# First block's second layer in seven block products, with weight sums prepared in four tiles and a newly computed order list

## The chip, the cores and the metric

The kernel runs on one core of one Trainium2 chip. The metric is the device time of that core in microseconds (us), a median over runs. TensorE (PE) multiplies, VectorE (DVE) and ScalarE (ACT) work on vectors, GpSimd (POOL) reduces over partitions and issues the large weight loads, SyncE (SP) issues smaller transfers.

## What is computed

Attention with a window of 64 positions, then two layers of a feed-forward network with a leaky rectifier between them, all in 32-bit floats:

```
scores = scale * q @ k.T            # 8 batches, 8 heads, 576 positions, head size 64
mask   = (rel >= 0) & (rel < 64)    # rel = query position - key position
attn   = softmax(where(mask, scores, -1e9));  x = (attn @ v) as 4608 tokens x 512
h = x @ w_in                        # 512 x 2048
g = maximum(0.01 * h, h)
out = g @ w_out                     # 2048 x 512
```

## The kernel before, in words

Every 32-bit number is held as a high and a low part, and a product is three matmuls of 128x128 weights on 128x512 columns (high by high, high by low, low by high). The attention works in 36 **units** of 128 queries, numbered m. The 4608 tokens are 9 chunks of 512: chunks 0 to 2 go through both layers plainly, and the other six are three **blocks** s = 0, 1, 2 of two chunks each.

The first layer of a block (lines 1318 to 1355, names `m0` to `m2`) is computed in seven products of half-size blocks in place of eight, which takes sums of weight blocks and of x blocks made beforehand. The second layer of blocks 1 and 2 (`second_in_seven`, line 1229, names `z1`, `z2`, line 1186) does the same with sums of the intermediate g and of `w_out`. The second layer of block 0 (lines 1361 to 1382, function `second`, line 1132, name `y0`) is computed plainly: 2 chunks by 16 slices of g by 4 output tiles by 3 matmuls.

In a second layer, ACT copies a wide piece of g (128x1024) into the high part of a *pair* tile (`wide_high`, line 1163), DVE writes the low part (`wide_low`, line 1167), and PE multiplies by it. In `y0` a pair serves 24 matmuls and there are two pair tiles (`gs` and `pxa`); in `z1` and `z2` a pair serves 12 matmuls and there are three (`third` besides). DVE also adds pieces of g there (`combine`, line 1170).

The sums of weights are made in `prepare` (line 1013): a fetch of the parts, on DVE one wide addition of high and low (line 1033, for `w_out` alone), four narrow additions (line 1036), a copy on ACT (line 1039), a subtraction on DVE (line 1042), a store. For `w_in` the fetch is of the whole numbers (`w_single`, stored by `split`, line 247, as the weights are converted at the start), for `w_out` of high and low parts (`w_second`).

A unit of the attention goes: scores on PE (line 278); mask on DVE (line 666, `shield_of`); for units from 20 on the result stays in the accumulator bank and ACT copies it (line 672, `held_back`); maximum over partitions on POOL (line 681); subtraction on DVE (line 688); exponential on ACT (line 692); sum on POOL (line 684); and the values on PE (line 740). Then come three transfers in a row on SP: the sums are compacted (`late_c<-late_o`, line 695), written as rows after a reciprocal (`rows<-late_c`, line 716) and spread again (`late_r<-rows`, line 728). The **normalisation** `product_of` (line 752, DVE) waits for the last of them, and its result is stored for the next block's x (`x_build`, line 852, loads it back and makes the sums of x).

From the start to the first layer of chunk 0 an order written out by hand is followed (`ORDER`, line 54). All later work is a list of operations, each with an engine, a duration and a rank; `arrange` (line 544) walks through it once, always taking the ready operation of lowest rank, and every engine executes its instructions in the order that comes out. Ranks of late units carry an added 0.45, and the waits of their transfers extra lags, for instance `lag=0.3 + 6 * late` before the normalisation (line 837).

Of the kernel before, what the change touches and what calls it, by code (L numbers as in the profile page):

```python
# [38 lines left out]
PACE = 2  # L39
LANES = 8  # L40
# [44 lines left out]
RING_AT = (5, 6, 7, 8)  # L85
HELD_FROM = 20
IN_PREP_AT = (0, 0, 0, 6, 7, 0, 6, 7)
OUT_PREP = 0.6
IN_SEVEN = (1, 2)
# [15 lines left out]
def band_attention_ffn(ctx: ExitStack, tc: tile.TileContext, qk, vW, vL, w_in, w_out, eye_mask, out, outT):  # L105
# [89 lines left out]
    w_single = dram.tile([FT, P, 512], F32, name="w_single")  # L195
# [336 lines left out]
    def op(engine, us, fn, *after, rank=1.0, lag=0.12, land=0.0):  # L532
        x = dict(engine=engine, us=us, fn=fn, after=[a for a in after if a], rank=rank, lag=lag, land=land, n=len(plan))
        plan.append(x)
        return x
# [8 lines left out]
    def arrange():  # L544
        free, left = dict.fromkeys(("PE", "DVE", "ACT", "POOL", "SP"), 0.0), list(plan)
        waiting = {e: [] for e in free}
        missing, users = {}, {}
        for x in plan:
            missing[x["n"]] = len(x["after"])
            for a in x["after"]:  # L550
                users.setdefault(a["n"], []).append(x)
            if not x["after"]:
                waiting[x["engine"]].append((0.0, x))
        order, landed = [], [0.0] * LANES

        def begins(ready, x):
            return max(ready, landed[0]) if x["land"] and x["engine"] != "POOL" else ready

        while any(waiting.values()):
            best = None  # L560
            for e, xs in waiting.items():
                if xs:
                    t = max(free[e], min(begins(*y) for y in xs))
                    if best is None or t < best[0]:
                        best = t, e
            t, e = best
            r, x = min((y for y in waiting[e] if begins(*y) <= t), key=lambda y: (y[1]["rank"], y[1]["n"]))
            waiting[e] = [y for y in waiting[e] if y[1] is not x]
            free[e] = t + x["us"]
            x["end"] = free[e] + x["land"]  # L570
# [4 lines left out]
            for y in users.get(x["n"], ()):  # L575
                missing[y["n"]] -= 1
                if not missing[y["n"]]:
                    at = max(a["end"] + (0.0 if a["engine"] == y["engine"] and not a["land"] else y["lag"]) for a in y["after"])
                    waiting[y["engine"]].append((at, y))
        assert len(order) == len(plan)  # L580
        return order

    MM, TWO, ONE, ACTS = 0.2267, 1.05, 0.72, 0.62
# [3 lines left out]
    XT_AT, PREP_AT = 4, 6  # L587
# [36 lines left out]
    turn_of = [15, 14, 13, 12] + list(range(12))  # L624
# [28 lines left out]
    stored = [(f, fn) for f in turn_of for fn in stores_of(f)]  # L653
# [14 lines left out]
    def held_back(m):  # L668
        return m >= HELD_FROM
# [101 lines left out]
    def attend(m, gate):  # L771

        soon = 0.35 if early(m) else 1.3
        o, late = at.setdefault(m, {}), 0.0 if early(m) else 0.45
# [23 lines left out]
        for j in range(2):  # L798
            o[f"A{j}"] = op("POOL", 3.5, partial(add_of, m, j), o[f"X{j}"], before.get(f"c{j}"), rank=0.4 + late)
# [7 lines left out]
    def normalise(m):  # L807

        late = 0.0 if early(m) else 0.45
        soon = 0.15 if early(m) and m > 13 else 0.8 + late  # L810
# [41 lines left out]
    def x_build(s, n, xt_of, xt_free, x_free):  # L852

        STEP, WIDTH = (0.42, 0.27) if s == 2 else (0.5, 0.35)
        urge, wait = ((0.2, 0.2), (1.4, 2.6), (0.6, 2.6))[s]
# [118 lines left out]
    for n, (c, f) in enumerate(walk):  # L974
        next_main(6 * MM, partial(early_first, n, 0), lows.get(n - 2), *ready[f], *(x2 if c == 2 else ()))
        first = next_main(6 * MM, partial(early_first, n, 1))
        if n == 0:
# [5 lines left out]
            gate = op("SP", 0.02, open_room, *all_in, s_free)  # L983
        if n > 1:
# [28 lines left out]
    def prepare(n, f, at, hurry, *freed):  # L1013
        def tile_of():
            return g_tile(at) if at else hold("spare", F32)
# [441 lines left out]
```

## Time and profile before

| what | value |
|---|---|
| median of 3 runs | 849.75 us (849.49 to 850.38) |
| span of the profiled execution | 849.6 us |
| PE busy | 842.2 us (99%), 6784 matmuls |
| DVE busy | 621.6 us (73%) |
| ACT busy | 375.3 us (44%) |
| POOL busy | 383.1 us (45%) |
| granted TensorE clock | full in every slice |
| moved by DMA | 226.80 MB, mean 267 GB/s |

A busy share is an average over stages with different limits. A span of a few hundred nanoseconds on PE is one matmul's time from issue to end, and neighbours overlap; the chain of waits gives the time from one to the next.

### The profile page before, as it was taken

The numbers are of one execution on the slowest core, as the hardware profiler recorded it, in microseconds if no ns is written. First come the engines' busy times: TensorE is split into PE (matmuls) and PEld (weight loads), VectorE is DVE, ScalarE is ACT, GpSimd is POOL, SyncE is SP. The second block draws the span as 40 slices with busy tenths as digits, with TensorE's granted clock in tenths as the row PEclk, the third lists the DMA queues.
The fourth block names the chain that finished last, engine by engine and source line by source line (L and its number), as shares of the span: only waits on it lengthen the run. The fifth ranks groups of instructions, "written<-read, shape, count | busy, mean of one in ns | idle before, by whom it ended". The sixth has DMA issues, their size and how long they took to land.

```text
span 849.6 us, 16804 instructions
## 1 busy us (share of the span) xinstructions
PE 842.2 (99%) x6784; PEld 686.8 (81%) x6784; DVE 621.6 (73%) x884; ACT 375.3 (44%) x605; POOL 383.1 (45%) x218
## 2 busy tenths in 40 slices
PE   9999999999999999999999999999999999999998
PEld 6887888888878888878888888888888888888887
DVE  6999885748768879857649977585679955546864
ACT  4665654333433444444444433444354533324431
POOL 5423000878888715578577857857111111111110
PEclk9999999999999999999999999999999999999999
DMA  9874756898899968999999999999997987777682
GB/s 326 271 235 146 252 165 232 264 289 269 283 318 323 306 200 286 298 309 329 320 328 364 375 355 316 361 317 304 247 270 234 248 247 199 198 197 192 192 214 96
DMA packets 127901, 226.80 MB, mean 267 GB/s; under 512 B 15568, under 2 KB 46672, under 8 KB 127824
## 3 DMA queue, kind: packets, MB, share of 16 engines
q0 software_dynamic: 51552, 90.18, 38.4%
q10 hardware_dynamic: 35664, 77.31, 27.8%
q1 hardware_dynamic: 40608, 58.24, 21.5%
q8 instruction: 53, 0.87, 0.4%
q14 instruction: 24, 0.20, 0.1%
HBM read 172.52 MB, written 53.06 MB: 266 GB/s over the span
## 4 chain that ended last, share of the span: by engine, by line
PE 91%; DVE 4%; DMA 4%; issue 0%; ACT 0%; SPq 0%; ACTq 0%; DVEq 0%
PE m L1118 25%; PE z L1186 18%; PE acc L929 11%; PE h L920 11%; PE y L1138 10%; PE h L431 4%; PE acc L467 4%; PE s L278 4%; PE o L740 3%; DMA late_r<-rows 1%; DMA raw<-w_out 1%; DMA rows<-late_c 1%; DMA raw<-w_in 1%; PE o L367 1%; DVE w L242 1%; DMA w_single<-w 0%
## 5 line engine op out<-in xcount | busy, mean ns | idle before, releaser
L1118 PE MATMUL m<-pfew,p 128*128 128x512 f32 x720 | 169.4, 391 | 0.0
L1118 PEld LDWEIGHTS m<-pfew,p 128*128 128x128 f32 x720 | 134.5, 188 | 28.3
L1102 POOL DMA_DIRECT2D p<-w_first x42 | 31.7, 755 | 114.2 <-PE m L1118 62.4
L929 PE MATMUL acc<-p,gs 128*128 128x512 f32 x324 | 80.6, 394 | 0.0
L1127 DVE TENSOR_TENSOR p<-m,pxa 128x512 f32<-128x512 f32 x60 | 41.4, 689 | 45.6 <-PE m L1118 45.2
L681 POOL PARTITION_ALL_REDUCE g<-late_f x20 | 36.8, 1874 | 79.4 <-DVE late_f L666 71.6
L1118 PE MATMUL m<-pxb,p 128*128 128x512 f32 x288 | 71.0, 392 | 0.7 <-DVE pxa L1127 0.7
L684 POOL PARTITION_ALL_REDUCE late_o<-late_f x20 | 65.3, 3290 | 11.6 <-ACT late_f L692 7.1
L929 PEld LDWEIGHTS acc<-p,gs 128*128 128x128 f32 x324 | 59.8, 188 | 12.8
L1130 ACT ACTIVATE p<-p 128x512 f32<-128x512 f32 x60 | 37.9, 631 | 72.7 <-DVE p L1127 72.5
L1127 DVE TENSOR_TENSOR pxa<-m,pxa 128x512 f32<-128x512 f32 x60 | 41.4, 689 | 37.1 <-PE m L1118 36.4
L1118 PEld LDWEIGHTS m<-pxb,p 128*128 128x128 f32 x288 | 53.6, 188 | 12.4 <-DVE pxa L1127 1.1
L684 POOL PARTITION_ALL_REDUCE late_o<-e x18 | 59.6, 3343 | 8.5 <-ACT e L692 4.1
L684 POOL PARTITION_ALL_REDUCE late_o<-late_e x18 | 59.2, 3315 | 5.8 <-ACT late_e L692 5.6
L1186 PE MATMUL z<-gs,p 128*128 128x512 f32 (+1 forms) x240 | 57.2, 386 | 0.0
L1102 POOL DMA_DIRECT2D p<-w_second x28 | 22.7, 810 | 72.2 <-PE z L1186 34.0
L920 PE MATMUL h<-pxa,p 128*128 128x512 f32 x228 | 54.9, 390 | 0.0
L1186 PEld LDWEIGHTS z<-gs,p 128*128 128x128 f32 x240 | 44.8, 188 | 9.2
L1186 PE MATMUL z<-pxa,p 128*128 128x512 f32 x216 | 52.0, 389 | 0.0
L1186 PE MATMUL z<-third,p 128*128 128x512 f32 x216 | 51.9, 389 | 0.0
L920 PEld LDWEIGHTS h<-pxa,p 128*128 128x128 f32 x228 | 42.6, 188 | 9.0
L1186 PEld LDWEIGHTS z<-third,p 128*128 128x128 f32 x216 | 40.5, 188 | 8.4
(197 smaller groups left out, 1750.1 us busy)
## 6 DMA issues: line engine op xcount, KB each, us to landing
p<-w_first POOLq DMA_DIRECT2D x42, 1024.0 KB, 6.9
p<-w_second POOLq DMA_DIRECT2D x28, 1024.0 KB, 8.5
p<-w_sums POOLq DMA_DIRECT2D x16, 1024.0 KB, 6.0
qk<-qk ACTq DMA_DIRECT2D x26, 512.0 KB, 6.1
pspare<-w_second ACTq DMA_DIRECT2D x16, 512.0 KB, 7.4
w_sums<-pspare ACTq DMA_DIRECT2D x16, 512.0 KB, 7.3
raw<-w_out ACTq DMA_DIRECT2D x15, 512.0 KB, 4.1
raw<-w_in ACTq DMA_DIRECT2D x14, 512.0 KB, 4.1
```

What stands on the lines that cost most here:

```text
L278: nc.tensor.matmul(ps[j][t, c : c + QB], k[i][s, p], q[s, w, p], start=not begun and (not more or (w, p) == (0, 0)), stop=not begun and no ...
L431: nc.tensor.matmul(ps, a[:, k, :], b[:, k, part], start=n == 0, stop=n == len(terms) - 1)
L681: nc.gpsimd.partition_all_reduce(most_of(j), e_of(m)[:, j], P, ReduceOp.max)
L684: nc.gpsimd.partition_all_reduce(sum_of(j), e_of(m)[:, j], P, ReduceOp.add)
L920: nc.tensor.matmul(ps, a[:, k, :], b[:, k], start=i == 0, stop=i == len(terms) - 1)
L929: nc.tensor.matmul(acc[c, i], a[:, i * P : (i + 1) * P], b, start=begin and k == 0, stop=n in ends and k == 2)
L1102: nc.gpsimd.dma_start(to, of, max_dma_last_dim=2048)
L1118: nc.tensor.matmul(tiles[b], w[:, 256 * i + 128 * kt : 256 * i + 128 * kt + 128], x_part(OF_X[k], j, kt), start=begin and c == 0, stop=c = ...
L1127: nc.vector.tensor_tensor(to(), tiles[b], x(), ALU.add)
L1130: nc.scalar.activation(to(), to() if b is None else tiles[b], AF.Prelu, alpha=0.01)
L1138: nc.tensor.matmul(tiles[i], a, b, start=f == 0 and k == 0, stop=f == FT - 1 and k == 2)
L1186: nc.tensor.matmul(tiles[b + i][:, cut], a, x[:, cut], start=begin and f == first and c == 0, stop=f == half - 1 and c == 2, skip_group_ch ...
```

## The change

1. Block 0's second layer goes through `second_in_seven` too (names `z0`). The products are taken in the order 0, 2, 1, 3, 4, 5, 6; its totals lie in two tiles of the attention's exponentials; the first eight pairs use two pair tiles, later ones three, the third being the tile `spare`. `second` and `put_out` are gone.
2. `w_single` holds the whole numbers of `w_out` too: `split` stores each converted weight tile, where it stored every other. `prepare` fetches them from there for both, and the wide addition is gone.
3. `prepare` works in four tiles (`spare`, a weight tile of slice 6 that is lent and loaded again before chunk 2 reaches slice 6, which now comes last, and two tiles of g). All sums of `w_out` are due before block 0's second layer.
4. Units 28 to 35 (`HALT`) wait at fixed points until block 0's second layer has freed their tiles, and are not held back: their masked scores go to SBUF at once.
5. `arrange` runs a forward pass, then eight times a backward pass, which gives every operation its latest start, and a forward pass in which all engines but PE take the ready operation with the earliest of these; the best order is kept. A resource `port` keeps DVE operations that read two SBUF operands and POOL's reductions apart. The added 0.45 and the lags that hung on it are zero.

The diff, cut to its core:

```diff
-RING_AT = (5, 6, 7, 8)
+RING_AT = (5, 7, 8, 6)
-IN_PREP_AT = (0, 0, 0, 6, 7, 0, 6, 7)
-OUT_PREP = 0.6
-IN_SEVEN = (1, 2)
+PREP = 0.4
+PASSES = 8
+LENT, LENT_TO = 6, 8
+PREP_AT = (None, "lent") * 4 + (6, 7, None, 6, 7, None, 6, 7)
+TWO_PAIRS = 8
+HALT = 28
...
     def split(n):
         nc.scalar.copy(flat(parts(n)[0]), singles[n])
-        if n % 2 == 0:
-            nc.scalar.dma_start(w_single[n // 2], singles[n])
+        nc.scalar.dma_start(w_single[n % 2, n // 2], singles[n])
...
+        port = {"POOL": {"max_of": 1.0, "add_of": 2.2}.get(named, 0.0), "DVE": us if named in SHARED else 0.0}.get(engine, 0.0)
...
+    def arrange():
+        for x in plan:
+            for a in x["after"]:
+                users.setdefault(a["n"], []).append(x)
+        best = now = forward(lambda x: x["rank"])
+        for _ in range(PASSES):
+            backward(now[0])
+            now = forward(lambda x: x["rank"] if x["engine"] == "PE" else x["late"])
+            best = min(best, now, key=lambda y: y[0])
+        return best[1]
...
     def held_back(m):
-        return m >= HELD_FROM
+        return HELD_FROM <= m < HALT
...
-        soon = 0.35 if early(m) else 1.3
-        o, late = at.setdefault(m, {}), 0.0 if early(m) else 0.45
+        soon = 0.35
+        o, late = at.setdefault(m, {}), 0.0
...
         def fetch(i):
-            if n:
-                to = tile_of()[:, 1024 * i : 1024 * (i + 1)].rearrange("p (j c) -> p j c", j=2)
-                nc.scalar.dma_start(to, w_second[:, f::half, 512 * i : 512 * (i + 1)])
-            else:
-                nc.scalar.dma_start(prep(0)[:, 2 * i : 2 * i + 2], w_single[f + half * i].rearrange("p (k c) -> p k c", k=2))
-
-        def whole_of():
-            nc.vector.tensor_tensor(prep(0), prep(0), prep(1), ALU.add)
+            nc.scalar.dma_start(prep(0)[:, 2 * i : 2 * i + 2], w_single[n, f + half * i].rearrange("p (k c) -> p k c", k=2))
...
+    def kind_of_pair(s, n):
+        return 2 * (n % 2) if s == 0 and n < TWO_PAIRS else n % 3
...
-        if s in IN_SEVEN:
-            second_in_seven(s)
-            continue
-        for t in range(2):
-            for f in (j * half + 2 * p + a for p in range(4) for j in range(2) for a in range(2)):
...
-                for i in range(4):
-                    after = bank_free[i] if f == 0 else ()
-                    next_main(3 * MM, partial(second, s, n, f, i, 2 * (q % 2), f"y{s}_{t}_{i}"), got, split_of[t, f], *after)
...
+        second_in_seven(s)
```

How the instructions move is shown at three places. The first is PE in block 0's second layer, where one pair tile (`pxa_38` before, `pxa_40` now) gives way to the other (`gs`); the tile behind the comma is the weights, and x3 means three matmuls of one output tile. Before:

```order
L1138 MATMUL y_0_1_4627<-pxa_38_4632,p_32_3609 128x512 x3
L1138 MATMUL y_0_2_4636<-pxa_38_4632,p_32_3609 128x512 x3
L1138 MATMUL y_0_3_4641<-pxa_38_4632,p_32_3609 128x512 x3
L1138 MATMUL y_0_0_4620<-gs_81,p_29_3452 128x512
L1138 MATMUL y_0_0_4620<-gs_82,p_29_3452 128x512
L1138 MATMUL y_0_1_4627<-gs_81,p_29_3452 128x512
```

Now:

```order
L1256 MATMUL z_0_0_4761<-pxa_40_4740,p_33_3622 128x512 x3
L1256 MATMUL z_0_1_4762<-pxa_40_4740,p_33_3622 128x512 x3
L1256 MATMUL z_0_0_4761<-gs_81,p_36_3819 128x512
L1256 MATMUL z_0_0_4761<-gs_82,p_36_3819 128x512
L1256 MATMUL z_0_1_4762<-gs_81,p_36_3819 128x512
```

A pair was read for four output tiles and two slices, 24 matmuls, and is read for two output tiles and two slices now, 12 matmuls. In the whole program the 384 matmuls of `y0` give way to 336 of `z0`.

The second place is DVE as block 0's second layer begins, around the subtractions of unit 27 (`e<-s,g`) and the normalisation of unit 25 (`late_n<-o,late_r`). Before:

```order
L666 SCALAR_TENSOR_TENSOR s_0_4668<-s_0_4668,away 128x512
L666 SCALAR_TENSOR_TENSOR s_1_4669<-s_1_4669,away 128x512
L688 TENSOR_TENSOR e<-s_0_4668,g 128x512
L1167 TENSOR_TENSOR pxa_38_4632<-p_37_4012,pxa_38_4632 128x1024
L688 TENSOR_TENSOR e<-s_1_4669,g 128x512
L752 TENSOR_TENSOR late_n<-o_4548,late_r 128x4x2x64
L703 RECIPROCAL late_c_1771<-late_c_1771 128x8
```

Now (line 1237 writes a low part, line 1240 adds pieces of g):

```order
L736 SCALAR_TENSOR_TENSOR s_1_4703<-s_1_4703,away 128x512
L1237 TENSOR_TENSOR pxa_40_4740<-p_39_4129,pxa_40_4740 128x1024
L1240 TENSOR_TENSOR p_39_4129<-pxa_35_3798,p_39_4129 128x1024
L758 TENSOR_TENSOR e<-s_0_4702,g 128x512
L773 RECIPROCAL late_c_1784<-late_c_1784 128x8
L822 TENSOR_TENSOR late_n<-o_4546,late_r 128x4x2x64
L1237 TENSOR_TENSOR gs_82<-p_25_3084,gs_81 128x1024
L758 TENSOR_TENSOR e<-s_1_4703,g 128x512
L1237 TENSOR_TENSOR pxa_40_4740<-p_24_3001,pxa_40_4740 128x1024
```

The normalisation of unit 25 stood behind both subtractions of unit 27 and stands between them now, directly ahead of the low part of the third pair.

The third place is ACT in the hand-written start, where weight tiles 10 and 11 are converted (a CAST), stored to `w_single` and the next raw weights are fetched. Before, with buffer numbers:

```order
L245 CAST p5_4_86<-w10_867 128x512
L247 DMA w_single_94<-w10_867 128x512
L210 DMA raw13_937<-w_out 128x1024
...
L245 CAST p5_4_86<-w11_948 128x512
L210 DMA raw14_953<-w_in 128x1024
```

Now:

```order
L250 CAST p5_4_86<-w10_871 128x512
L251 DMA w_single_94<-w10_871 128x512
L215 DMA raw13_942<-w_out 128x1024
...
L250 CAST p5_4_86<-w11_953 128x512
L251 DMA w_single_94<-w11_953 128x512
L215 DMA raw14_959<-w_in 128x1024
```

Tile 11 has a store of its own now, which ACT issues between its conversion and the fetch of raw tile 14.

## Rows read from the trace of the kernel before

**Rows 1.** From the page's first two parts: engines with busy us, share of the span and instructions; then the granted TensorE clock in tenths, in 40 slices of the span.

```profile
PE 842.2 (99%) x6784; PEld 686.8 (81%) x6784; DVE 621.6 (73%) x884; ACT 375.3 (44%) x605; POOL 383.1 (45%) x218
PEclk9999999999999999999999999999999999999999
```

**Rows 2.** Idle time of PE and what ended it, whole execution: us in total, times, longest us.

```profile
PE m L1118 <- DVE pxa L1127: 0.7, 1, 0.7
PE s L312 <- DVE pxb L401: 0.7, 1, 0.7
```

**Rows 3.** The chain that ended last: a unit's scores and values in `y0`, then all of `z1` and nearly all of `z2`: start us, us to the next piece, what.

```profile
452.32 1.09 PE s L278 x64
453.41 1.08 PE o L740 x32
...
617.82 76.16 PE z L1186 x336
...
770.14 75.53 PE z L1186 x336
```

**Rows 4.** The stages of chunks 0 to 2, `m0`, `y0` and `z1`, with their start and end and length in us: busy us (and instructions) of PE, weight loads, DVE, ACT, POOL; granted clock; DMA share; GB/s.

```profile
129.00:341.20 212.20, 212.20 (x2094) 171.79 (x2093) 157.74 (x207) 86.55 (x155) 135.89 (x56) 1.00 0.85 278
341.20:430.90 89.70, 88.98 (x817) 72.90 (x818) 62.13 (x92) 40.78 (x73) 62.91 (x36) 1.00 1.08 315
430.90:532.60 101.70, 101.70 (x961) 83.67 (x960) 81.47 (x101) 42.22 (x64) 74.06 (x40) 1.00 1.14 349
617.80:694.00 76.20, 76.20 (x338) 63.10 (x337) 64.07 (x75) 37.34 (x44) 10.96 (x14) 1.00 0.91 251
```

**Rows 5.** DVE operations by line and form, mean ns of one behind the busy us: low parts (1167) and the wide addition in `prepare` (1033).

```profile
L1167 DVE TENSOR_TENSOR gs<-p,gs 128x1024 fp32r<-128x1024 f32 x27 | 36.3, 1343 | 14.8 <-ACT gs L1163 14.7
L1167 DVE TENSOR_TENSOR pxa<-p,pxa 128x1024 fp32r<-128x1024 f32 x23 | 34.4, 1495 | 16.3 <-ACT pxa L1163 16.3
L1033 DVE TENSOR_TENSOR pspare<-pspare 128x1024 f32<-128x1024 f32 x8 | 12.5, 1564 | 0.3 <-DMA pspare<-w_second 0.3
```

**Rows 6.** Line 1167 by itself: durations in ns, least, median and longest of one.

```profile
L1167 DVE TENSOR_TENSOR gs<-p,gs x27: 1211/1224/3344, 363.3 to 839.3; 128x1024 fp32r<-128x1024 f32 x27
```

**Rows 7.** ACT and DVE as `z1` begins, in order of time: start us, us.

```profile
623.20 1.22 DVE L1170 TENSOR_TENSOR p<-p 128x1024 f32<-128x1024 f32 x1
623.30 1.06 ACT L1163 CAST third<-p 128x1024 fp32r<-128x1024 f32 x1 [1.61 <-PE z L1186]
624.38 1.22 DVE L1167 TENSOR_TENSOR third<-p,third 128x1024 fp32r<-128x1024 f32 x1
```

**Rows 8.** The chain around 61 us, in the start: start us, us, what.

```profile
60.88 0.70 DVE w L242
...
61.61 6.54 DMA raw<-w_in
...
68.18 0.43 DVE raw L225
68.61 0.61 DVE pxb L401
...
69.26 0.73 PE s L312 x2
```

**Rows 9.** The stores to `w_single`: time on the issuing queue in ns, and time from issue to landing of what touches `w_single`, us.

```profile
L247 ACTq DMA_DIRECT2D w_single<-w x16: 332/333/527, 13.4 to 144.4; - x16
DMA to landing us min/median/max: 2.0/4.8/8.5
```

**Rows 10.** Unit 25 and, for unit 27, scores and subtraction: from the chain and the engines' timelines, start us, us.

```profile
405.62 1.09 PE s L278 x64
413.32 6.40 POOL L684 PARTITION_ALL_REDUCE late_o<-late_e x2
436.98 1.09 PE s L278 x64
441.84 0.69 DVE L688 TENSOR_TENSOR e<-s,g 128x512 f32<-128x512 f32 x1 [1.99 <-POOL g L681]
447.08 0.68 DVE L752 TENSOR_TENSOR late_n<-o,late_r 128x512 f32<-128x512 f32 x1
```

**Rows 11.** Time from issue to landing of the three transfers ahead of a normalisation, in their order: lines 695, 716, 728.

```profile
DMA to landing us min/median/max: 1.9/5.3/8.9
DMA to landing us min/median/max: 2.2/5.3/8.5
DMA to landing us min/median/max: 3.1/6.0/9.0
```

**Rows 12.** The chain in `m0` up to PE's one wait there: start us, us, what.

```profile
362.48 7.99 DMA late_r<-rows
...
370.59 0.09 DVE late_n L752
...
371.20 0.69 DVE pxa L1127
```

**Rows 13.** POOL's reductions, durations of one in ns: the maximum (681) and the sum (684); then the weight loads issued on POOL with their mean.

```profile
L681 POOL PARTITION_ALL_REDUCE g<-late_f x20: 1740/1860/2301, 149.4 to 581.0; - x20
L684 POOL PARTITION_ALL_REDUCE late_o<-late_f x20: 3182/3272/3523, 153.5 to 587.3; - x20
L1102 POOL DMA_DIRECT2D p<-w_first x42 | 31.7, 755 | 114.2 <-PE m L1118 62.4
```

More of the change, by code (lines that the diff above doesn't have):

```diff
@@ L1 @@
 import math
+from bisect import bisect_left, insort
 from contextlib import ExitStack
@@ L39 @@
 PACE = 2
+SHARED = ('minus_of', 'low_early', 'rest', 'join', 'sign', 'wide_low', 'combine', 'sub', 'low', 'join_of', 'product_of')
 LANES = 8
@@ L541, in bulk, with gap_of, forward @@
         return op("ACT", 0.5, fn, *after, rank=rank, lag=lag, land=land)
-    def arrange():
-        free, left = dict.fromkeys(("PE", "DVE", "ACT", "POOL", "SP"), 0.0), list(plan)
+    users = {}
+    def gap_of(a, x):
+        return 0.0 if a["engine"] == x["engine"] and not a["land"] else x["lag"]
+    def forward(urgency):
+        free = dict.fromkeys(("PE", "DVE", "ACT", "POOL", "SP"), 0.0)
         waiting = {e: [] for e in free}
-        missing, users = {}, {}
+        missing = {x["n"]: len(x["after"]) for x in plan}
         for x in plan:
-            missing[x["n"]] = len(x["after"])
-            for a in x["after"]:
-                users.setdefault(a["n"], []).append(x)
             if not x["after"]:
                 waiting[x["engine"]].append((0.0, x))
-        order, landed = [], [0.0] * LANES
+        order, landed, port = [], [0.0] * LANES, 0.0
         def begins(ready, x):
+            if x["port"]:
+                return max(ready, port)
             return max(ready, landed[0]) if x["land"] and x["engine"] != "POOL" else ready
@@ L577, in arrange @@
                 if not missing[y["n"]]:
-                    at = max(a["end"] + (0.0 if a["engine"] == y["engine"] and not a["land"] else y["lag"]) for a in y["after"])
-                    waiting[y["engine"]].append((at, y))
+                    waiting[y["engine"]].append((max(a["end"] + gap_of(a, y) for a in y["after"]), y))
         assert len(order) == len(plan)
-        return order
-    MM, TWO, ONE, ACTS = 0.2267, 1.05, 0.72, 0.62
+        return max(x["end"] for x in plan if x["engine"] == "PE"), order
@@ new lines, in lent, with take_back, reload @@
+    def lent():
+        if held.get("lent") is None:
+            held["lent"] = place(LENT, F32)
+        return held["lent"]
+    def take_back():
+        held["back"] = t = place(LENT, F32R).rearrange("p (i c) -> p i c", i=4)
+        both[LENT] = t.bitcast(F32)
+        wi[LENT] = [t[:, i].rearrange("p (a b) -> p a b", a=KT) for i in range(2)]
+        wo[LENT] = [t[:, 2 + i] for i in range(2)]
+    def reload(of, cut):
+        if "back" not in held:
+            take_back()
+        nc.scalar.dma_start(both[LENT][cut], of)
@@ L1158, in wide_pair @@
         if "third" not in held:
-            held["third"] = [wk.tile([P, 1024], F32R, tag="raw", bufs=3, name=f"third{i}") for i in range(2)]
-        return held["third"]
+            held["third"] = place("spare", F32R)
+        return held["third"][:, :1024], held["third"][:, 1024:]
     def wide_high(s, n, t, j, p):
```

228 lines of the change are left out of this document (132 added, 96 removed).

## The prediction, made before the changed kernel was timed

> **What bounds the kernel now.** I read the page's shares first: PE is busy for 99% of the span, at the granted clock of its full level (2.4 GHz) in every slice [rows 1]. A busy PE could still be a slow one, so the second view is who made PE wait: after the start there is one wait of 0.7 us, in `m0` [rows 2]. The third is the table of stages: in chunks 0 to 2, in `y0` and in `z1` the busy time of PE equals the stage's length, and `m0` lacks just those 0.7 us [rows 4]. The fourth is the chain that ended last, where `z1` is one piece of 336 matmuls in 76.16 us [rows 3], so 76.16/336 = 0.2267 us from one matmul to the next. From 129 us to the end PE is the bound, and a matmul less is 0.2267 us less, as long as the other engines still keep up. The profiled execution took 849.6 us, 0.15 us under the median of 849.75; the sum below is made against 849.6. About 0.2% (1.7 us) is what a measurement of this kernel can tell from no change.
>
> **The change part by part.**
>
> *Fewer products.* Block 0's second layer goes from 2 x 16 x 4 x 3 = 384 matmuls to 7 x 8 x 2 x 3 = 336. That is 48 x 0.2267 = 10.9 us, all on the path. The units' scores (1.09 us) and values (1.08 us) [rows 3] stay as many; they only change places, so PE's other work is unchanged.
>
> *Half as much PE work behind each pair.* In `y0` a pair covered 24 matmuls (5.44 us), in `z0` it covers 12 (2.72 us). `z1` lives with 2.72 us, but with three pair tiles; the first eight pairs of `z0` have two. With two, a pair must be refilled while PE multiplies by the other: copy 1.06 us, hand-over 0.02 us, low part 1.22 us [rows 7], 2.3 us of 2.72. It fits by 0.4 us if DVE stands ready. Six refills happen so, and the order puts one other DVE operation of 0.7 to 1.2 us ahead of about half of them, so each of these is late by 0.3 to 0.8 us. A unit's scores and values in between (2.2 us) give two refills air. Bounds: 0, and six refills each behind one operation of 1.22 us, 7.3 us. I take 1.5 us.
>
> *DVE as a whole in this stage.* `z1` has 75 DVE operations of 64.07 us in 76.2 us [rows 4]. `z0` has the same lows and combinations, and about ten more of about 0.7 us (subtractions, masks, normalisations, two additions that ACT made as copies): 64 + 7 = 71 us. PE needs 76.16 us plus three pieces of units, 3.3 us, so 79.4 us. DVE is at 90%. It fits, and costs nothing by itself; the 10% that is left is the cover of the term before.
>
> *The weight sums.* Eight wide additions (1.56 us each [rows 5], 12.5 us of DVE) go, and half of the `w_out` fetches' bytes. The rest moves from all over the run into chunk 2 and `m0`. In chunks 0 to 2 DVE was busy for 157.7 of 212.2 us, in `m0` for 62.1 of 89.7 [rows 4]; some 20 us more in the two together leaves both under 85%. DMA in `m0` is the tighter side, with 315 GB/s against 349 in `y0` [rows 4]; it was carried there without a wait of PE, so I add nothing. If that cover is gone, late sums hold up the weight loads of product 3 in `z0`, which the ring of four loads gives some 16 us. The tile lent to the sums is loaded again about 70 matmuls (16 us) ahead of its use: nothing.
>
> *The start.* Sixteen more stores of converted weights. ACT issues them in its own stream, 0.33 us each [rows 9]. One place is on the path: weight tile 11 is joined at 60.88 us, raw tile 14 is fetched at 61.61, and DVE stands until it lands, ahead of the operation that lets PE go on at 69.26 [rows 8]. The new store of tile 11 is issued just ahead of that fetch, so 0.33 us, and its 256 KB run beside it. A join must also wait for the store of two tiles before, which takes 2.0 to 8.5 us [rows 9]; of the odd tiles 5, 9 and 11 are near that. Bounds: 0, and 3 us (a store 4 us over the middle row, less about 1 us of slack). I take 0.6 us.
>
> *Normalisations.* DVE works in order, so a normalisation whose rows have not landed holds the low parts behind it. This is what made PE's one wait: `late_r` took 7.99 us, the normalisation came at 370.59, the addition behind it at 371.20, PE after that [rows 12]. The extra lags that kept it away from its transfers are zero now, and units come closer: 31.4 us for two before [rows 10], 28.8 now (below). Unit 25 is the closest: its scores came at 405.62, its sums ended at 419.72 and its normalisation ran at 447.08, 41.5 us after the scores [rows 10]. Now it stands behind the first subtraction of unit 27. Between the scores of 25 and of 27 the new order has 108 matmuls and two units' pieces, 24.5 + 4.3 = 28.8 us; from unit 27's scores to the end of its first subtraction it took 441.84 + 0.69 - 436.98 = 5.6 us [rows 10]. It is due 34.4 us after its scores. Its transfers can land 14.1 us (sums) + 5.3 + 5.3 + 6.0 by the middle rows [rows 11], and about 1.2 for two small operations and the second issue: 31.9 us. By the longest rows it is 14.1 + 8.9 + 8.5 + 9.0 + 1.2 = 41.7 us. So it is 2.5 us early in the middle and up to 7.3 late. Units 24 to 27 are all close; a wait for one gives the next the same time, so they don't add. Bounds: 0 and 9 us. I take 1.0 us, and 0.5 us more for units 28 to 35 in `m1` (bounds 0 and 4), where POOL has 2 x 1.86 + 2 x 3.27 + 2.25 loads x 0.76 = 12.0 us of work per unit [rows 13] in 14.4.
>
> *The old wait* of 0.7 us in `m0` was one normalisation at its place in the old order. New waits of that kind are in the terms above, so the old one is taken out once.
>
> *The port.* Low parts take 1224 ns in the middle, up to 3344 [rows 6], with means of 1343 and 1495 [rows 5] where POOL was reducing beside them: 27 x 0.12 + 23 x 0.27 = 9.4 us over the run, most of it in `y0`, where some 22 reductions ran, 0.4 us for each. In `z0` six reductions run, 2.6 us of DVE, half of it hidden; it is within the 1.5 us above. The Trainium skill, page "SBUF — State Buffer", section "Who interferes with whom", has a harder rule: a DVE instruction with two SBUF inputs and a GpSimd instruction that reads SBUF lock each other out for a whole instruction. The longest row agrees with it, the middle one shows that most operations meet no reduction.
>
> **Sum.** 849.6 - 10.9 - 0.7 + 1.5 + 0.6 + 1.0 + 0.5 = **841.6 us**. With all costs at zero it is 838.0; I set the low end at 838.6, since one of them will show.
>
> **The rivals.**
>
> *Half is given back (844 to 848 us).* Refills and normalisations cost near their upper bounds in `z0`: 5 us for refills and 3 for normalisations in place of 2.5 together, so about 847. For it: two pair tiles, 90% of DVE, lags at zero. Against: the one wait of 0.7 us in 720 us shows that an order computed from such durations holds on the chip.
>
> *The lock decides (about 848.5 us).* Unit 27's four reductions lie beside the first four pairs. If each blocks one low part for the excess of the longest row, 3.34 - 1.22 = 2.1 us, PE stands 8.4 us in place of 1.5. For it: that row. Against: 0.4 us per reduction in `y0`.
>
> *Slower (about 854 us).* The normalisations become the bound. In `m0`, `z0` and `m1`, 16 units are normalised; at most every second counts, since a wait for one gives time to the next. If their transfers land near the longest rows, each of eight holds DVE and PE 2 us: 838.0 + 8 x 2 = 854.0. It decides from (11.6 + 1.7)/8 = 1.7 us each on: 11.6 us are won by matmuls and the old wait, and 1.7 can be told. For it: [rows 12] and 7.3 us at the longest. Against: less is moved in `z0`, as `z1` shows with 251 GB/s [rows 4], and PE has a few matmuls of cover in `m0` and `m1`.
>
> **How the numbers follow.** Forecast case (838.6 to 844) 0.60; half given back 0.25; lock 0.08, half of it beyond 848; slower 0.07. Faster by over 0.2% (below 848.0): 0.60 + 0.25 + 0.03 = 0.88, of which I give 0.02 to causes that I have not seen, so 0.86. Slower by over 0.2%: 0.07. Within: 0.07. The range is 838.6 to 847.5: the first two cases and little of the third, leaving out about 0.15.
>
> **What would show it.** Right: 336 matmuls of `z0` in place of 384 of `y0`; PE without a wait in `z1`, `m2` and `z2`; `z0` some 79 to 83 us long. The refills: PE waits on the low parts (line 1237) in the first eight pairs, under 1 us each. The start: the first long run of PE begins 0 to 1.5 us later than 69.26. The normalisations: idle time of DVE ahead of line 822, ended by `late_r<-rows`, followed by a wait of PE, for units 24 to 27. Wrong: waits of PE over 5 us in `m0`, `z0` or `m1`; or low parts of 3 us in `z0`; or PE held in `z0` by weight loads that wait for `w_sums`.

## The result, and the profile after

| | before | changed |
|---|---|---|
| median time | 849.88 us (849.49 to 850.38, 4 runs) | 857.72 us (856.53 to 857.87, 4 runs) |
| span of the profiled execution | 849.6 us | 856.0 us |

The ratio is 1.0086, interval 1.0074 to 1.0099: 0.86% slower, where 841.6 us was forecast, 8.0 us under the span of before. A time is some 1.8 us more than its span (857.77 us with 856.0); I had put the span of before, 849.6, beside the times, so its profiled execution was not level with the median but some 1.5 us over it.

The page's first part of the changed kernel, as [rows 1]: engines with busy us, share of the span, instructions.

```profile
PE 836.3 (98%) x6736; PEld 678.9 (79%) x6736; DVE 637.4 (74%) x912; ACT 377.8 (44%) x599; POOL 383.3 (45%) x216
```

The 48 matmuls are gone, but PE is busy for 5.9 us less, not 10.9, and the span has 19.7 us without PE where it had 7.4. Who made PE wait, as [rows 2]: us in total, times, longest us.

```profile
PE z L1256 <- DVE gs L1237: 4.2, 1, 4.2
PE z L1256 <- DVE pspare L1237: 1.9, 1, 1.9
PE s L316 <- DVE pxb L405: 1.8, 2, 0.9
PE m L1190 <- DVE pxa L1199: 1.8, 1, 1.8
...
PE z L1256 <- ACT pxa L1233: 1.1, 1, 1.1
PE h L990 <- DVE gs L1010: 1.1, 1, 1.1
PE z L1256 <- DVE pxa L1237: 0.8, 1, 0.8
```

The stages `m0`, `z0`, `m1` and `z1`, as [rows 4]: start and end, length, then busy us (and instructions) of PE, weight loads, DVE, ACT, POOL; granted clock; DMA share; GB/s.

```profile
344.79:437.59 92.80, 91.05 (x914) 74.56 (x912) 66.65 (x103) 44.45 (x77) 72.06 (x39) 1.00 1.10 328
437.59:527.22 89.63, 83.53 (x501) 67.88 (x497) 76.49 (x89) 38.78 (x48) 25.19 (x19) 0.96 0.89 255
527.22:620.08 92.86, 92.86 (x945) 75.26 (x943) 64.73 (x87) 35.44 (x62) 77.03 (x42) 1.00 0.90 255
620.08:699.86 79.78, 77.92 (x373) 64.03 (x369) 69.47 (x81) 36.95 (x46) 20.79 (x17) 1.00 0.92 258
```

`z0` stands out: 6.1 us without PE, and a granted clock of 0.96, the only stage under 1.00. The chain that ended last shows how the longest wait came about (start us, us, what):

```profile
431.59 3.32 POOL late_o L754
434.91 0.02 issue
434.93 0.47 SPq L765
435.40 0.05 issue
435.45 0.02 SPq L798
...
436.09 8.24 DMA late_r<-rows
...
444.41 0.69 DVE late_n L822
445.10 2.64 DVE gs L1237
447.74 0.04 issue
447.79 1.22 PE z L1256 x2
```

DVE (first fence) and POOL (second) at that place, in order of time, with idle time and its releaser in brackets:

```profile
440.95 0.68 DVE L758 TENSOR_TENSOR e<-s,g 128x512 f32<-128x512 f32 x1
441.91 0.20 DVE L773 RECIPROCAL late_c<-late_c 128x8 f32<-128x8 f32 x1 [0.28 <-ACT late_c L769]
444.41 0.69 DVE L822 TENSOR_TENSOR late_n<-o,late_r 128x512 f32<-128x512 f32 x1 [2.29 <-DMA late_r<-rows]
445.02 2.72 DVE L1237 TENSOR_TENSOR gs<-p,gs 128x1024 fp32r<-128x1024 f32 x1
```

```profile
444.46 3.18 POOL L754 PARTITION_ALL_REDUCE late_o<-e  x1
```

ACT, which writes the high part that the low part is taken from:

```profile
440.72 1.06 ACT L1233 CAST gs<-p 128x1024 fp32r<-128x1024 f32 x1 [1.71 <-PE z L1256]
```

And what the clock did: first PE's wait, then the 13 matmuls behind it (columns as in the stages).

```profile
443.50:447.80 4.30, 0.09 (x2) 0.02 (x1) 3.39 (x3) 0.98 (x1) 3.95 (x2) 0.86 1.21 331
447.80:453.10 5.30, 5.30 (x13) 4.19 (x14) 1.66 (x2) 0.79 (x2) 3.41 (x1) 0.50 0.88 283
```

Read upwards from PE: it waits for a low part of `gs`, whose high part was there at 441.78 us (copied in 1.06 from 440.72). DVE stood ahead of it for 2.29 us at the normalisation of unit 25, since the rows landed at 444.33. Their transfer of 8.24 us was issued at 436.09: on SP it stood behind the compaction of unit 26, which waited for POOL's sum to end at 434.91, though its own source had landed at 433.6. The low part then took 2.72 us in place of 1.22, beside the next sum, and ended 0.1 us after it. PE, 4.21 us late, went on at half clock (1.2 GHz) for 13 matmuls, 2.7 us more. So behind 2.29 us of an idle DVE stand 6.9 us of PE, of which the low part's meeting with the sum makes 1.5 and the clock 2.7.

The same happens at the normalisation of unit 21 in `m0`, and once, in chunk 1, with the low part of unit 8's x (line 837), which writes where blocks of `out` have not yet left. DVE's waits for transfers:

```profile
DVE late_n L822 <- DMA late_r<-rows: 11.7, 8, 3.5
DVE pxa L837 <- DMA out<-pxa: 7.9, 1, 7.9
...
DVE w L247 <- DMA w_single<-w: 2.2, 2, 1.9
```

**Where the time went**, both traces cut at the same instruction (88.17 us before, 90.31 after; before that point the start is 2.1 us longer). I took each step from one matmul's start to the next at 0.2267 us, idle time apart as waits, what is above the rate in steps over 0.26 us as slow steps, and the steps through units by themselves:

| from the cut to the last matmul, us | before | after | difference |
|---|---|---|---|
| steps at the rate | 674.9 | 663.3 | -11.6 |
| PE waits | 0.7 | 10.8 | +10.1 |
| slow steps (half clock and steps beside a break) | 5.3 | 9.6 | +4.3 |
| units' scores and values | 76.3 | 77.2 | +0.9 |

With the start (2.1), 0.2 of shorter steps and 0.3 us behind the last matmul that is, but for rounding, +6.4, the difference of the spans. The matmuls were saved; of the 18 us that were lost, waits, slow steps and the start are 16.5.

### The profile page after: what moved, and what is told of

Read it like the earlier page. It is cut to its first block, busy times and chain, and to the rows that moved or that the text cites. A ratio compares the mean times of both kernels' runs of the same rounds, so it can differ in the third digit from the quotient of the medians.

```text
span 856.0 us, 16720 instructions
## 1 busy us (share of the span) xinstructions
PE 836.3 (98%) x6736; PEld 678.9 (79%) x6736; DVE 637.4 (74%) x912; ACT 377.8 (44%) x599; POOL 383.3 (45%) x216
## 4 chain that ended last, share of the span: by engine, by line
PE 84%; DMA 7%; DVE 4%; POOL 2%; issue 2%; ACT 1%; SPq 1%; ACTq 0%; DVEq 0%; POOLq 0%
PE z L1256 26%; PE m L1190 22%; PE acc L999 10%; PE h L990 10%; PE h L435 4%; PE acc L471 4%; PE s L282 3%; PE o L810 3%; DMA late_r<-rows 2%; DMA raw<-w_out 1%; DMA w_single<-w 1%; POOL late_o L754 1%; DMA rows<-late_c 1%; DMA out<-pxa 1%; PE o L371 1%
## 5 line engine op out<-in xcount | busy, mean ns | idle before, releaser
L1256 PE MATMUL z<-gs,p 128*128 128x512 f32 (+1 forms) x372 | 91.9, 396 | 4.2 <-DVE gs L1237 4.2
L1256 PE MATMUL z<-pxa,p 128*128 128x512 f32 x348 | 84.8, 392 | 1.9 <-ACT pxa L1233 1.1
L1256 PEld LDWEIGHTS z<-gs,p 128*128 128x128 f32 x372 | 70.8, 192 | 19.5 <-DVE gs L1237 4.6
L1256 PEld LDWEIGHTS z<-pxa,p 128*128 128x128 f32 x348 | 65.5, 189 | 16.3 <-ACT pxa L1233 1.6
L1256 PE MATMUL z<-pspare,p 128*128 128x512 f32 x288 | 69.5, 389 | 1.9 <-DVE pspare L1237 1.9
L754 POOL PARTITION_ALL_REDUCE late_o<-e x18 | 60.6, 3380 | 16.6 <-ACT e L762 12.7
L1256 PEld LDWEIGHTS z<-pspare,p 128*128 128x128 f32 x288 | 54.0, 188 | 13.5 <-DVE pspare L1237 2.3
L1174 POOL DMA_DIRECT2D p<-w_sums x24 | 18.0, 748 | 103.6 <-PE z L1256 93.6
```

The lines of the kernel that those rows point to most:

```text
L754: nc.gpsimd.partition_all_reduce(sum_of(j), e_of(m)[:, j], P, ReduceOp.add)
L1174: nc.gpsimd.dma_start(to, of, max_dma_last_dim=2048)
L1256: nc.tensor.matmul(tiles[b + i][:, cut], a, x[:, cut], start=begin and f == first and c == 0, stop=f == half - 1 and c == 2, skip_group_ch ...
```

## The experiments

Two theories stood against each other: A, a few DVE operations stand ahead of work that PE waits for, before their transfers have landed; B, the shared port and a DVE that is too full in `z0` set the pace. For the start: the stores cost what they cost by waits for a buffer, or by their bytes. Times are medians; ratios are to the kernel before on the same chip (the changed kernel: 1.0086).

### The normalisations

**moved**: the order that comes out of `arrange` is kept but for two operations on DVE.

```diff
+    later_place(order_of, 21, 2)
+    later_place(order_of, 25, 2)
```

> The changed kernel with one thing moved: on DVE the normalisation of unit 21 stands behind one addition of m0 that stood behind it, and that of unit 25 behind one low part of z0 (gs) that stood behind it; nothing else moves on any engine. Theory A (normalisations placed ahead of work that PE waits for, before their rows have landed, cost most of the loss): the PE waits of 1.75 us in m0 and 4.21 us in z0 go, with them the stretch of 2.7 us at half clock; a wait of 0 to 1.5 us for the next low part may come in z0. 856.0 - 1.9 - 4.2 - 2.7 + 0 to 1.5 = 847 to 849 us of span, so 5 to 9 us less than the changed kernel, about level with the kernel before. Rival B (the shared port and a DVE that is too full in z0 set the pace): PE waits as long a few operations later, less than 2 us are won, 854 to 856 us. Rival C (the transfers themselves hold up more than these two places): waits turn up for units 22 to 27, 2 to 4 us are won.

Measured: 852.25 us, ratio 1.0030 (1.0014 to 1.0046); span 850.6. One place each, and some 5 us are back. `m0` has no wait, the 4.21 us and the half clock are gone. A wait of 1.49 us came for the next low part, beside the same sum of POOL (DVE of moved):

```profile
441.89 1.17 DVE L1237 TENSOR_TENSOR gs<-p,gs 128x1024 fp32r<-128x1024 f32 x1
444.11 0.69 DVE L822 TENSOR_TENSOR late_n<-o,late_r 128x512 f32<-128x512 f32 x1 [1.05 <-issue]
444.72 0.68 DVE L758 TENSOR_TENSOR e<-s,g 128x512 f32<-128x512 f32 x1
445.32 2.28 DVE L1237 TENSOR_TENSOR pxa<-p,pxa 128x1024 fp32r<-128x1024 f32 x1
```

Theory A holds for these two places; B is in what is left.

**nowait**:

```diff
+        if HELD_FROM <= m < HALT:
+            nc.vector.tensor_tensor(by_unit(done_of(m)), x, by_unit(done_of(m + 1)), ALU.subtract)
```

> The changed kernel, order unchanged; the normalisations of units 20 to 27 subtract the result tile of the neighbouring unit in place of multiplying by the spread sums, so that they wait for no transfer (this leaves out the division of those units). Theory A: the PE wait in m0 (1.75 us) goes; in z0 DVE reaches the low part of gs 2.3 us earlier, ahead of POOL's sum, and the wait of 4.21 us falls under 1.5, no half clock: 847 to 850 us. Rival B: the low part still ends with POOL's sum at its old place, PE waits 3 us or more in z0 and at most 2 us are won in all, those of m0: 854 us.

Measured: 852.47 us, ratio 1.0038 (1.0023 to 1.0053). The kernel leaves out the division of units 20 to 27. The wait in `m0` is gone; in `z0` 4.21 us became 0.28 and 0.88. Two edits that have only the wait in common win the same.

**lags**:

```diff
-lag=0.3 + 6 * late
+lag=0.3 if early(m) else 3.0
```

(ahead of guards and of normalisations.)

> The changed kernel with the planner's lags ahead of guards and normalisations of units from 20 on at 3.0 us, as before the change, in place of 0.3. The whole order is worked out anew. Theory A: DVE's waits for late_r ahead of the normalisations fall from 11.7 us in 8 places to under 4, the PE waits in m0 and z0 to under 2 us together, no half clock in z0; 847 to 850 us. Rival B (port and DVE load in z0): waits of PE on low parts remain 3 us or more, 853 us or more. The start (about 1.9 us later than before) and the wait of 1.1 us in chunk 1 stay under either theory.

Measured: 855.64 us, ratio 1.0066 (1.0054 to 1.0078). For theory A a miss by 6 us: DVE's waits for `late_r` fell from 11.7 to 0.9 us and `m0` has 0.4 us, but the new order has its own waits, 2.9 us at a unit's values in chunk 1 and 2.2 us for a low part in `z0`, and it keeps 1.1 and 0.9 us at a later pair there. What rival B forecast came out: PE waits 3.2 us for low parts in `z0`, and the time is over 853. The 2.2 us need no late transfer. A combination (line 1240) stood ahead of that low part and met a sum of POOL, with which it ended (DVE and POOL of lags):

```profile
441.68 3.37 DVE L1240 TENSOR_TENSOR p<-pxa,p 128x1024 f32<-128x1024 f32 x1
441.78 3.18 POOL L754 PARTITION_ALL_REDUCE late_o<-e  x1
```

Lags cure the place, not the order as a whole.

### The start

**oddhigh** reads the stored odd tiles from a place that no join needs:

```diff
-        nc.scalar.dma_start(w_single[n % 2, n // 2], singles[n])
+        nc.scalar.dma_start(w_single[n % 2, n // 2], flat(parts(n)[0]).bitcast(F32) if n % 2 else singles[n])
```

> The changed kernel, order unchanged; the stores of odd weight tiles to w_single read the high part of the tile, which stays in place, in place of the joined tile whose buffer the join of two tiles later takes (the sums of w_out are then made of high parts). The store's bytes, its issue on ACT and its time stay. Theory S1 (the joins wait for the odd stores to land): DVE's 2.2 us of waiting for w_single go, the first long run of PE begins at 69.3 to 70 us in place of 71.2, 1.2 to 1.9 us are won: 854 to 855 us. Rival S2 (the issue on ACT and the bytes beside the raw fetches cost it): start within 0.4 us of the changed kernel's, under 0.5 us won.

Measured: 856.78 us, ratio 1.0092 (1.0069 to 1.0115); the long run of PE begins at 70.50 us. DVE's waits for `w_single` fell from 2.2 to 0.5 us, and no gain can be told.

**nostores**:

```diff
+        if n % 2 == 0 or n // 2 >= half:
+            nc.scalar.dma_start(w_single[n % 2, n // 2], singles[n])
...
-w_single[n, f + half * i]
+w_single[n * i, f + half * i]
```

> The changed kernel, order unchanged, without the stores of the odd weight tiles 1 to 15, those of the start; the sums of w_out take parts of w_in tiles in their place (fetches as many and as large). Theory S1 (these stores cost the start what they cost the kernel before in run stores, 3.5 us): the long run of PE begins at 68.5 to 70 us in place of 71.2 to 72.5, 2.5 to 4 us less than the changed kernel, 853.5 to 855.5 us. Rival S2 (in the changed kernel something else takes their place, as the other changes of the order in the start): under 1 us less.

Measured: 854.83 us, ratio 1.0043 (1.0028 to 1.0058), 2.9 us less by the medians, as the first theory said. The long run of PE begins here (the chain of nostores):

```profile
69.06 0.73 PE s L317 x2
```

**stores** puts the other side to the test:

```diff
-        if n % 2 == 0:
-            nc.scalar.dma_start(w_single[n // 2], singles[n])
+        nc.scalar.dma_start((w_odd if n % 2 else w_single)[n // 2], singles[n])
```

> The kernel before with the 16 stores of odd weight tiles alone added (into a tensor that nothing reads). Theory S1 (the stores make the start of the changed kernel later, since a join waits until the store of two tiles before has landed): DVE waits on w_single come up, the long run of PE that began at 69.26 us begins 1.2 to 3.2 us later, 851 to 853 us. Rival S2 (the later start of the changed kernel is the spread of single executions): within 0.5 us of the kernel before.

Measured: 853.44 us, ratio 1.0040 (1.0026 to 1.0053). The stores alone, in the kernel before, cost 3.5 us; PE's run begins at 73.84 us in the chain of stores:

```profile
73.84 0.74 PE s L312 x2
```

**stores_high** is stores with the edit of oddhigh.

> Run stores (the kernel before with 16 stores added) with one difference: the added stores read the high part of the tile, which stays, so that no join waits for them to land. Bytes, issues and times of the stores are the same. If the loss of 3.5 us in stores comes from joins that wait for a buffer: within 1 us of the kernel before, 850 to 851 us. If it comes from the bytes beside the raw fetches and the issue on ACT: 852.5 to 854 us, as stores. Half and half is possible (run oddhigh won 0.9 us of median).

Measured: 852.78 us, ratio 1.0032 (1.0020 to 1.0043): its interval overlaps that of stores, so no share of the buffer is shown. The joins wait for no added store here, only 0.7 us for the even ones, as in before, and most of the loss is still there.

**before_again**, without an edit.

> The kernel before once more, for a second profile of its start. If the profiled execution of before (span 849.6 us, time 1.8 us more) was a late one in the start, the long run of PE that began at 69.26 us begins at 67 to 68.5 us here and the span is 847.5 to 848.5; else both are as there.

Measured: 850.42 us, span 848.6; the run begins at 69.04 us. So the start of before is steady: 69.26 and 69.04, and 69.06 in nostores. With the odd stores on ACT it began between 70.50 and 73.84 in each of twelve kernels (71.19 in the changed one). The span of before was not long in the start; 0.7 of the 1.0 us between the two spans is its wait in `m0`, which before_again does not have.

**stores_sp** issues the added stores of stores on SP (`nc.sync`).

> Run stores (the kernel before with 16 stores added) with the added stores issued on SP in place of ACT; they read the joined tile as in stores. Theory Q (a raw fetch lands late because it stands behind a store of 256 KB in ACT's queue): the start comes back to 69 to 70.5 us, within 1.5 us of the kernel before, 850 to 851.5 us. Theory B (4 MB more beside the raw fetches, whatever the queue): 852 to 854 us as in stores and stores_high.

Measured: 861.95 us, ratio 1.0147 (1.0133 to 1.0161). Neither theory: SP works in order too, and loads of q and k stood behind stores that waited for their tiles. The chain of stores_sp:

```profile
67.93 0.25 SPq L247
68.18 0.05 issue
68.22 0.03 SPq L174
```

PE then waited for such loads, the last of them (`qk<-qk`, 7.86 us) up to 78.14. Bytes or position in a queue is not settled by it.

### The pairs in `z0`

**turn** adds to moved:

```diff
+        return 2 * (n % 2) if s == 0 and n < TWO_PAIRS else (n + (s == 0)) % 3
```

(for the tile alone; the order is worked out with the old turn, so in places a pair of `z0` is written before its tile has been read for the last time by the program's order, and other data is multiplied.) The rule of the changed kernel gives the eighth pair 2 x (7 mod 2) = 2 and the ninth 8 mod 3 = 2, both `pxa`.

> The kernel of run moved, order unchanged, with one thing more: from the ninth pair of z0 on the pair tiles are taken one place further in their turn (gs, spare, pxa), so that the eighth and the ninth pair no longer share the tile pxa. Theory A (the waits of 1.14 and 0.76 us at 464 and 465 us come from that shared tile: copy and low part can only begin when PE has done with the eighth pair): both go, 1.5 to 2 us less than moved, 848 to 849 us of span if the start is as in moved (850.6). Rival B (DVE, busy without a break from 457 to 475 us in the changed kernel, is the bound there): the waits stay at 1 us or more in all or turn up at the next pairs, under 0.8 us won.

Measured: 853.33 us, ratio 1.0044 (1.0028 to 1.0060). The waits of 1.14 and 0.76 us went, and 0.87 and 1.99 us came at 458 and 466 us. Rival B was right here: in the changed kernel DVE is busy from 457 to 471 us but for 1.1 us, and the tile's turn alone wins nothing.

**three**:

```diff
-TWO_PAIRS = 8
+TWO_PAIRS = 0
```

> The changed kernel with three pair tiles from the first pair of z0 on (two for the first eight pairs before); the whole order is worked out anew from it. Theory A (two tiles and their change-over cost the PE waits on pairs in z0, beside the normalisation of unit 25): PE's waits on pairs in z0 fall from 6.1 us to under 2, no half clock, 848 to 851 us. Rival B (DVE's work in z0 is the bound whatever the tiles): waits of 4 us or more in z0 remain, 853 us or more. Under either, the start stays some 2 us later than before and the wait in chunk 1 may stay.

Measured: 852.50 us, ratio 1.0028 (1.0010 to 1.0046). PE waits for no pair in `z0`. Its waits are elsewhere: 2.0 us in `m0` and 1.7 us in `m1`, and 2.0 us in chunk 1.

**three_y30** adds a lag of 3.0 ahead of the late normalisations alone.

> As three, and with the planner's lag ahead of the normalisations of units from 20 on at 3.0 us in place of 0.3. If zero lags and two tiles are the two causes in m0 and z0, PE's waits from m0 on fall under 2 us in all, 845 to 849 us, at or below the kernel before. If the waits are only moved to m1 and m2 by the new order, 850 to 854 us.

Measured: 848.91 us, ratio 0.9991 (0.9981 to 1.0002): level with the kernel before. From `m0` on PE waits 2.2 us in all. Two more waits stand in chunks 1 and 2, 2.0 and 1.0 us, and the low part of x waits 8.4 us on DVE.

### What was left

**evenstart** is three_y30 without the whole odd tiles 1 to 13:

```diff
+        if n % 2 == 0 or n // 2 >= 7:
...
+            nc.vector.tensor_tensor(prep(0)[:, :2], prep(1)[:, :2], prep(1)[:, 2:], ALU.add)
```

> Run three_y30 with the odd weight tiles of the start (1 to 13) not stored whole; their parts for the sums of w_out are fetched as high and low parts and added on DVE (7 additions of about 0.7 us), all numbers as in the reference. The order is worked out anew. If the start's stores cost what run stores shows (3.5 us) and the rest stays as in three_y30 (848.9): 845 to 847 us, faster than the kernel before by 0.4 to 0.6%. If the additions and the later fetches hold up the sums at the end of m0: 848 to 851 us.

Measured: 851.95 us, ratio 1.0017 (1.0000 to 1.0034). A miss: PE's run began at 70.10 us, but the additions made another order, with 2.2 us of waits in chunk 1, 3.1 late in `m0` and 1.5 in `z0`.

**three_sp** is three_y30 with odd stores on SP.

> Run three_y30 (848.9) with the stores of odd weight tiles issued on SP; order otherwise unchanged. Theory Q: the start is 1.5 to 3 us earlier, 846 to 847.5 us, faster than both kernels. Theory B: 848 to 849.5 us.

Measured: 860.48 us, ratio 1.0127 (1.0111 to 1.0143), for the reason of stores_sp.

**three_placed** adds one line to three_sp:

```diff
+    later_place(order_of, at[8]["kept"][0], 7)
```

> Run three_sp with one operation moved on DVE: the low part of x of unit 8 (line 837), which stood idle for 8.4 us until blocks of out had landed, stands seven operations later. If that place costs what PE's waits at 203 us show (2.0 us), 1 to 2 us less than three_sp; if PE only waits a little later for something else, under 0.5 us less.

Measured: 856.81 us, ratio 1.0077 (1.0064 to 1.0091), 3.7 us less than three_sp. The wait of 2.5 us in chunk 1 is gone, with 0.95 us of slow steps behind it.

**placed** is three_y30 with that line, the stores on ACT.

> Run three_y30 (848.9; stores on ACT again) with the low part of x of unit 8 seven operations later on DVE, as in three_placed. Since that place made 3.7 us between three_sp and three_placed: 844.5 to 847 us, faster than the kernel before by 0.4 to 0.6%. If it was worth that much only because the start was late in those two: 847.5 to 849 us.

Measured: 846.37 us, ratio 0.9954 (0.9941 to 0.9966): faster than both kernels.

**deferred** is placed with each odd store of the start issued behind the next raw fetch:

```diff
-        nc.scalar.dma_start(w_single[n % 2, n // 2], singles[n])
+        unsent.append(partial(nc.scalar.dma_start, w_single[n % 2, n // 2], singles[n]))
```

> Run placed, with the store of each odd weight tile of the start issued on ACT behind the next raw fetch (or ahead of the next join), not ahead of it; bytes and queue stay. If the start is late because a raw fetch stands behind a store in the queue: 1 to 3 us less than placed. If the bytes are what costs: within 1 us of placed, and a join may wait longer for its buffer.

Measured: 844.91 us, ratio 0.9943 (0.9930 to 0.9957), the fastest of all, though not apart from placed by its interval; its start is still late (71.80 us). Two of its PE waits, in the start and in `z0`, and the stages `m0` to `z1`:

```profile
PE s L324 <- DVE pxb L413: 2.4, 2, 1.8
...
PE z L1264 <- DVE pxa L1245: 0.8, 2, 0.5
```

```profile
343.95:432.70 88.75, 88.75 (x818) 72.64 (x816) 67.23 (x102) 43.46 (x76) 70.51 (x37) 1.00 1.13 338
432.70:516.42 83.72, 82.91 (x593) 67.78 (x592) 73.50 (x87) 38.57 (x48) 21.99 (x20) 1.00 0.98 277
516.42:607.75 91.33, 91.33 (x913) 74.60 (x912) 68.57 (x88) 33.87 (x61) 83.39 (x43) 1.00 0.90 254
607.75:686.52 78.77, 78.77 (x401) 64.96 (x400) 70.22 (x82) 38.42 (x48) 19.17 (x18) 1.00 0.95 269
```

PE is busy for the length of each stage but 0.8 us in `z0`, at full clock. Between the cut and the last matmul this kernel has 0.8 us of waits, where the changed one has 10.8.

## Why the prediction was wrong, point by point

The forecast was 8.0 us under the span of before; the change came out 6.4 over it by the spans, 7.8 by the medians.

| term | forecast | measured | where |
|---|---|---|---|
| fewer products | -10.9 | -10.9 | 48 fewer, each at 0.2267 |
| old wait in `m0` | -0.7 | -0.7 | it is gone (also from before_again) |
| pairs of `z0` | +1.5 | +1.9 | 1.1 + 0.8 at the ninth pair, which takes the tile of the eighth |
| start | +0.6 | +1.9 in the trace, 2.9 by nostores | line 316 at 71.19 us, before 69.26 |
| normalisations, 24 to 27 | +1.0 | 6.9 | 4.2 us of wait, 2.7 us of half clock, unit 25 |
| normalisation, unit 21 | in no term | 2 | 1.8 us of wait in `m0`, and the step beside it |
| units in `m1` | +0.5 | 0 | DVE waits there, PE does not |
| x of unit 8, chunk 1 | in no term | 1.1 | line 837 behind 7.9 us of DVE's waiting |
| pairs of `z1` | in no term | 1.9 | the order: a combination and another low part ahead of `pspare`'s |

The rows add up to 4.1 us; of the other 2.3 of the 6.4 us, 1.4 are single slow steps beside breaks, the rest lies in pieces of 0.3 us or less. A sign that I had named as wrong was there: `z0` has 6.1 us of waits, over 5. What the sum said of the matmuls holds: `z0` without its waits and the 2.7 us of half clock is 80.8 us long, within 79 to 83, and deferred, which lacks those waits, has a span of 842.6 us, 1.0 over the forecast.

The step that failed most is the value for the **normalisations**. The place was named, unit 25, and its bounds of 0 and 9 us held what it cost; I took 1.0. The due time was fair (34.4 us after the scores; DVE stood there after some 36). The landing was not: 31.9 us from middle rows, 38.2 measured. The sums came 1.0 us later than before, 15.1 us after the scores. The transfers took 6.5, 3.6 and 8.2 us, near the middle in sum, 18.3 against 16.6. The rest was queues: 1.9 us on SP behind the compaction of unit 26 and 0.6 behind the first half of the same rows, and 2.1 us at the guard (line 769, ACT) and the reciprocal before the second issue, where I had 1.2 for all of this. I priced the late landing alone, and not what follows a wait: the low part met a sum of POOL (1.5 us) and PE came back at half clock (2.7 us). Unit 21 I left out, though [rows 12] showed one such wait in `m0`; I even wrote it off with the old order.

The **pairs of `z0`** came out near their number by luck. I had priced refills that stand behind another operation of DVE in the first eight pairs; apart from unit 25's place none of them made PE wait. The 1.9 us lie at the change from two tiles to three, which I had not looked at: two pairs in a row use `pxa`, so the copy on ACT (1.1 us of wait) and the low part (0.8) came only after PE had done with the pair before.

The **start** came out at the upper end of its bounds, 2.9 of 3. I weighed one store on the chain; six of the added ones lie in the first 72 us, and where they cost is not settled.

The **argument that an order computed from such durations holds on the chip** failed. It rested on one wait in 720 us of before. The waits on pairs at 469 and 641 us come back in moved and nowait to 0.01 us, so they belong to the order; three has none of them, and lags keeps the two in `z0` (1.14 and 0.91 us) and loses the one in `z1`. "DVE at 90% fits" was an average: from 457 to 471 us it has 1.1 us to spare, and turn shows that nothing is won there without another order.

Rivals: *slower* came true, for its named reason in part. It asked for eight units at 2 us each; two units and their consequences were enough, with the start. *Half is given back* had the right terms the wrong way round: 5 us for refills and 3 for normalisations, where 1.9 and some 9 came. *The lock* is seen: the low part of 2.72 us at 445.02 ends 0.1 us after POOL's sum, as do those of 3.54 us at 548.33 and 3.42 us at 632.46. The Trainium skill, page "SBUF — State Buffer", section "Who interferes with whom", says that a DVE instruction with two SBUF inputs contends with a GpSimd instruction that reads SBUF, and calls the ports that they share an exclusive lock. These three rows agree with that. Not every row does: a low part at 571.30 us took its usual 1.22 us beside the last 0.7 us of a sum (568.78 to 572.01). And the low parts at 548.33 and 632.46 began 0.27 and 0.16 us ahead of their sums and still ended with them, so by these rows it isn't always the later of the two that waits. As a rival it is refuted in part: moved and nowait, in which the lock stays, win 5 us, so in the changed kernel it lengthened waits and was not their main cause; in lags it made one of 2.2 us.

Not settled: bytes or queue position in the start; the wait in `z1`, which no run took away by itself (three_y30, placed and deferred do not have it).

## What to carry to other kernels

An operation that waits for a transfer blocks all that stands behind it on an engine that works in order: compare its place with the longest landing, the queue in which the transfer is issued included, and price what comes after the wait as well. Before believing an order that is computed, look for the two or three such operations ahead of work that the bounding engine needs; a longer lag ahead of one kind, seven places for another and a third tile turned +0.9% into -0.5%. An added transfer in a busy start costs there, even if nothing reads it: 3.5 us in stores.

## What the runs showed of the hardware

The clock after short waits is not the same each time. After 4.21 us of wait it was granted at 0.50 (above), and so it was in nostores and oddhigh, which have the same wait; each lost 2.4 to 2.8 us by it. At the waits of 1.14 and 0.76 us in `z0` nowait had half clock for eight matmuls, and moved had none at the same place (first nowait, then moved, columns as in the stages):

```profile
466.20:469.20 3.00, 3.00 (x8) 2.34 (x9) 2.97 (x6) 0.00 (x0) 0.00 (x0) 0.53 1.01 317
```

```profile
466.20:469.20 3.00, 3.00 (x13) 2.50 (x14) 2.97 (x6) 0.17 (x1) 0.00 (x0) 1.00 1.03 317
```

At the one wait of 1.85 us in `z1` it is the same: nowait, nostores and oddhigh had half clock for some eight matmuls behind it, the changed kernel, moved and turn had none (first nowait, then the changed kernel):

```profile
640.90:643.90 3.00, 3.00 (x8) 2.32 (x7) 2.35 (x4) 0.98 (x1) 0.59 (x1) 0.50 0.29 97
642.83:645.83 3.00, 3.00 (x13) 2.50 (x14) 3.00 (x5) 0.17 (x1) 0.00 (x0) 1.00 0.14 36
```

So 2 us of waits can cost 1.3 to 1.6 us more, or not, and times of kernels with such waits spread wider: moved from 849.02 to 856.12 us over nine runs, deferred from 844.42 to 845.54 over five. In moved the mean granted clock goes with the time: 1.000 in four runs of 849.02 to 852.17 us, 0.996 in the two longest.
